# A planner that knows when VectorE and GpSimd block each other, and that plans TensorE's attention products later

## The chip, the core and the metric

The kernel runs on one core of one Trainium2 chip. The metric is the device time of one execution in microseconds (us), as the median of several runs. The engines named below are TensorE (PE in the profile, with its weight loads as PEld), VectorE (DVE), ScalarE (ACT), GpSimd (POOL) and SyncE (SP), which here only issues transfers. Each engine works through its own instructions in their order; an instruction that waits for another engine holds up all that stand behind it on its own.

## The reference: what is computed

Sliding-window attention (8 batches, 8 heads, 576 positions, head dimension 64, window 64), whose output goes as 4608 tokens of 512 features through a feed-forward layer with a rational activation. All is float32.

```python
scores = np.where((rel >= 0) & (rel < 64), scale * q @ k.T, -1e9)
attn = softmax(scores)                     # exp(scores - max) / (sum + 1e-9)
x = (attn @ v), heads side by side         # 4608 x 512
h = x @ w_in                               # 4608 x 2048
P = a[0] + a[1] * h + a[2] * h2 + a[3] * h3
Q = 1.0 + abs(b[0]) * abs(h) + abs(b[1]) * h2
out = (P / (Q + 1e-6)) @ w_out             # 4608 x 512
```

## The kernel before

**Tiles.** The tokens are cut into 12 chunks of 384. Of each chunk, attention makes x in four *units* (`plan_unit`), one per pair of heads. The feed-forward layer then goes over the chunk in 16 *steps* (`plan_gate`, `plan_out`), one per 128 of the 2048 inner features: 192 steps in all. Chunks 0 to 2 take their first eight steps first and the other eight afterwards, since the weights are still arriving and being decoded; their partial outputs are spilled and merged. From chunk 3 on a chunk takes its 16 steps in one go.

**Three products for one.** TensorE multiplies a number as the sum of a high and a low part. So x is kept as xh and xl, the gate as gh and gl, the weights as wi_h, wi_l, wo_h, wo_l, and each product is made of three matmuls. The weights come as 64-bit numbers and are decoded (`plan_decode`) by two ScalarE operations, one of GpSimd (L237) and three of VectorE (L241, L246, L257) for each of 32 tiles.

**A unit** goes: scores on TensorE into the PSUM tile ps_s (L335); masked to SBUF by VectorE (sm, L341; in chunks 1 and 2 the mask is added by TensorE instead, L327); maxima (nmx, VectorE, L352); six exponentials with sums (ScalarE, L364); inverse sums (rs, VectorE, L368 and L369); normalisation of sm (GpSimd, L373); six transposes on TensorE, again into ps_s (L378); their copy pT to SBUF (ScalarE, L382); 24 small products with V into ps_x (TensorE, L388); xh (ScalarE, L393) and xl (VectorE, L397).

**A step** goes: twelve h products into the PSUM tile h, of which there are two buffers (TensorE, L437); ah = |h|, a first num and a first u (ScalarE, L443, L446, L449); num times h twice (VectorE, L452, L455: the last reader of h); u times ah (GpSimd, L459); logarithm and exponential of u, which make 1/Q in ah (ScalarE, L462, L465); gh, a product u, the remainder num, and gl = num times ah (VectorE, L469, L473, L477, L482); then nine o products, three for each of three token tiles, of gl and gh with the output weights, into PSUM tiles that hold the sum over the chunk's 16 steps (TensorE, L520). The buffers for gh and gl number three, for ah, u and num two.

**What sets the order.** No loop does: each operation is registered in a `Plan` with its engine, a planned duration, a rank, what it comes after and which buffers it takes. `Plan.order` then plays the program through with these durations. Again and again it looks at every engine for the operations whose buffers and inputs are there, takes those that could start within 0.02 us of the earliest, among these the lowest rank, and of all engines the one that starts first. Operations are issued in the order of their planned starts. The plan decides only the order: on the chip each instruction waits on semaphores for what it needs. So a planned duration that is wrong makes an order that fits the chip less well, and never a wrong result.

**What the plan knows of VectorE and GpSimd.** Some VectorE operations (three of the decode, gh, the product u, the remainder num) are marked `shares`. Where GpSimd is busy when such an operation is to start, half of the overlap is added to its duration. gl (L482) and all others are planned at their bare duration.

Of the kernel before, what the change touches and what calls it, by code (L numbers as in the profile page):

```python
# [27 lines left out]
class Slot:  # L28


    def __init__(self, pool):
        self.pool, self.uses = pool, []


class Op:
    def __init__(self, engine, cost, rank, emit, after, uses, shares):
        self.engine, self.cost, self.rank, self.emit, self.after, self.shares = engine, cost, rank, emit, after, shares
        self.start = self.end = None
        self.takes = [s for s in uses if not s.uses]
        for s in uses:  # L40
            s.uses.append(self)


class Plan:
# [9 lines left out]
    def add(self, engine, cost, rank, emit, after=(), uses=(), shares=False):  # L54
        op = Op(engine, cost, rank, emit, [o for o in after if o is not None], list(uses), shares)
        self.ops.append(op)
        return op

    def order(self):
# [8 lines left out]
        held = {}  # L68
# [5 lines left out]
        while len(done) < len(self.ops):  # L74
            best = None
            for e in ENGINES:
                able = []
                for op in ready[e]:
                    if any(not slots[s.pool] for s in op.takes):
                        continue  # L80
                    t = max([free[e], op.ready] + [min(slots[s.pool]) for s in op.takes])
                    able.append((t, op))
                if not able:
                    continue
                t0 = min(t for t, _ in able)
                t, op = min(((t, op) for t, op in able if t <= t0 + 0.02), key=lambda x: (x[1].rank, x[0]))
                if best is None or t < best[0]:
                    best = t, op
            t, op = best
# [4 lines left out]
            if op.shares and free["POOL"] > t:  # L94
                cost += 0.5 * min(cost, free["POOL"] - t)
            op.start, op.end = t, t + cost
            if op.engine == "SP":
                self.bus = max(t, getattr(self, "bus", 0.0)) + op.cost
                op.end = self.bus + 2.0
                free["SP"] = t + 0.06  # L100
            else:
                free[op.engine] = op.end - self.TAIL[op.engine]
# [20 lines left out]
def swa_rational_ffn(ctx: ExitStack, tc: tile.TileContext, qT, kT, v, w_in, w_out, a, b, out):  # L123
# [79 lines left out]
    HA = 8  # L203
    NU = HP
# [15 lines left out]
    def plan_decode(src, hi, lo, rank):  # L220
# [41 lines left out]
        o = plan.add("POOL", 1.75, rank, sign, [o], [st])  # L262
        o = plan.add("DVE", 0.685, rank, put_sign, [o], [st, sc], True)
        o = plan.add("DVE", 0.685, rank, put_low, [o], [st, sc], True)
        o = plan.add("ACT", 0.635, rank, high, [o], [sc])
        return plan.add("DVE", 0.685, rank, rest, [o], [sc], True)
# [14 lines left out]
    def plan_unit(c, hp, rank):  # L281
# [118 lines left out]
        def link(kind, op):  # L400
            chain[kind] = op
            return op
# [11 lines left out]
        o = plan.add("POOL", 1.58, r(6), normalise, [o], [ssm])  # L414
        o = link("transposes", plan.add("PE", 0.82, r(7), transposes, [o, chain.get("transposes")], [ssm, spt]))
        o = plan.add("ACT", 0.8, r(8), copy_pT, [o], [spt, spT])
        o = plan.add("PE", 1.1, r(9), values, [o, lv, chain.get("values")], [svt, spT, spx])
# [9 lines left out]
    def plan_gate(s):  # L427
# [63 lines left out]
        u_1 = plan.add("POOL", 1.035, r(5), u1, [u_0], [st])  # L491
        o = plan.add("ACT", 0.527, r(6), logarithm, [u_1], [st])
        o = plan.add("ACT", 0.527, r(7), inverse, [o], [st])
        g = plan.add("DVE", 0.615, r(8), g_high, [o, n2], [st, sg], True)
        o = plan.add("DVE", 0.56, r(9), product, [g], [st, sg], True)
        o = plan.add("DVE", 0.615, r(10), remainder, [o], [st], True)
        gate_done[s] = plan.add("DVE", 0.555, r(11), g_low, [o], [st, sg])
# [6 lines left out]
    def plan_out(s):  # L504
# [38 lines left out]
        for t in range(NTS):  # L543
            o = plan.add("PE", 0.855, s + LAG + 0.5 + 0.01 * t, lambda t=t: products(t),
                         [gate_done[s], tile_out[i], f2.get((s - 1, t)), f2.get((s, t - 1))], [sg, so[t]])
# [84 lines left out]
```

## Time and profile before

| | |
|---|---|
| median of 3 runs | 1034.44 us (1034.14 to 1034.7) |
| the profiled execution | 1032.78 us, of which the span from first to last instruction is 1030.8 us |
| mean granted TensorE clock | 0.982 |
| busy, share of the span | TensorE 93%, weight loads 80%, VectorE 87%, ScalarE 70%, GpSimd 36% |
| gl on VectorE (L482), 192 times | mean 930 ns |
| num times h on VectorE (L452), same size, 192 times | mean 546 ns |
| normalisation on GpSimd (L373), 48 times | mean 1630 ns |
| u on GpSimd (L459), 192 times | mean 1221 ns |

The profile is that of one execution. A row of a group names the line, the engine, the operation, the tile written and the tiles read, the number of instructions, their busy time, the mean of one, and the time for which the engine stood idle just before them with what ended the wait. Matmuls overlap each other, so the starts of successive matmuls tell more than the length of one. The lines of the changed kernel are eight higher than those before from the middle of the file on: L382 before is L390 after.

### The profile page before, as it was taken

What the parts mean: (1) busy time and instruction counts of PE and PEld (TensorE: products, weight loads), DVE (VectorE), ACT (ScalarE), POOL (GpSimd) and SP (SyncE); (2) the same over time, 40 slices, a digit from 0 to 9 for tenths busy, and PEclk for the clock granted to TensorE, in tenths of its full rate; (3) what the DMA queues carried; (4) which work ended last, traced back from release to release, by engine and by line L of the source; (5) the groups of instructions that cost most, each with busy time, mean ns of one, the idle gap of its engine ahead of it and who ended that gap; (6) DMA issues with size and microseconds to landing.
All of it is one profiled execution on the core that took longest, in us unless ns stands there. A gap on an engine that the chain in (4) does not pass through costs nothing.

```text
span 1030.8 us, 18377 instructions
## 1 busy us (share of the span) xinstructions
PE 961.4 (93%) x6640; PEld 829.2 (80%) x6640; DVE 899.2 (87%) x1538; ACT 724.8 (70%) x1735; POOL 371.1 (36%) x287
## 2 busy tenths in 40 slices
PE   4687999989999999999999999999999999999998
PEld 3566788868888888888888788888888888888997
DVE  5699999999998888888888888888888888888896
ACT  4685887767786677667767766766767776767665
POOL 4445544453233333233333333333333333332221
PEclk9598999989999999999999999999999999999999
DMA  5635424221232102111111111111211111200000
GB/s 188 188 121 150 158 80 128 62 62 45 75 122 73 47 33 69 42 44 59 44 34 43 61 46 50 62 37 37 76 30 43 63 45 33 79 16 1 32 1 31
DMA packets 39545, 67.24 MB, mean 65 GB/s; under 512 B 4640, under 2 KB 25120, under 8 KB 39456
## 3 DMA queue, kind: packets, MB, share of 16 engines
q1 hardware_dynamic: 39456, 66.08, 20.1%
q8 instruction: 52, 0.85, 0.3%
q14 instruction: 37, 0.30, 0.1%
HBM read 55.05 MB, written 11.01 MB: 64 GB/s over the span
## 4 chain that ended last, share of the span: by engine, by line
DVE 33%; PE 13%; ACT 13%; POOL 11%; issue 7%; DVEq 0%; POOLq 0%; ACTq 0%
POOL u L459 8%; PE h L437 6%; DVE gh L469 6%; PE o L520 6%; DVE u L473 6%; DVE num L477 4%; DVE gl L482 4%; DVE num L455 3%; POOL sm L373 3%; DVE sm L341 3%; ACT ah L465 3%; ACT ah L443 3%; DVE nmx L352 3%; ACT pT L382 2%; ACT ah L462 2%
## 5 line engine op out<-in xcount | busy, mean ns | idle before, releaser
L459 POOL TENSOR_TENSOR u<-u,ah 128x384 f32<-128x384 f32 x192 | 234.5, 1221 | 433.2 <-ACT u L449 388.4
L437 PE MATMUL h<-xl,wi_h 128*128 128x384 f32 x768 | 262.0, 341 | 5.1 <-ACT wi_h L254 2.9
L437 PE MATMUL h<-xh,wi_l 128*128 128x384 f32 x768 | 260.0, 339 | 1.2 <-DVE wi_l L257 1.2
L437 PE MATMUL h<-xh,wi_h 128*128 128x384 f32 x768 | 259.6, 338 | 0.0
L462 ACT ACTIVATE ah<-u 128x384 f32<-128x384 f32 x192 | 101.0, 526 | 216.1 <-POOL u L459 215.9
L520 PE MATMUL o<-wo_h,gl 128*128 128x512 f32 x576 | 238.9, 415 | 6.9 <-ACT wo_h L254 4.9
L520 PE MATMUL o<-wo_l,gh 128*128 128x512 f32 x576 | 228.2, 396 | 4.5 <-DVE wo_l L257 4.4
L520 PE MATMUL o<-wo_h,gh 128*128 128x512 f32 x576 | 228.3, 396 | 0.0
L469 DVE SCALAR_TENSOR_TENSOR gh<-num,a_sb,ah 128x384 fp32r<-128x384 f32 x192 | 123.2, 642 | 78.3 <-ACT ah L465 70.0
L482 DVE TENSOR_TENSOR gl<-num,ah 128x384 fp32r<-128x384 f32 x192 | 178.5, 930 | 2.2
L437 PEld LDWEIGHTS h<-xl,wi_h 128*128 128x128 f32 x768 | 145.7, 190 | 18.1 <-DVE num L455 5.2
L437 PEld LDWEIGHTS h<-xh,wi_h 128*128 128x128 f32 x768 | 145.7, 190 | 7.1
L373 POOL TENSOR_TENSOR sm<-sm,rs 128x768 f32<-128x768 f32 x48 | 78.3, 1630 | 194.0 <-DVE rs L369 175.3
L437 PEld LDWEIGHTS h<-xh,wi_l 128*128 128x128 f32 x768 | 145.5, 189 | 2.2 <-DVE wi_l L257 2.2
L520 PEld LDWEIGHTS o<-wo_h,gl 128*128 128x128 f32 x576 | 108.6, 189 | 34.0 <-ACT wo_h L254 5.6
L449 ACT ACTIVATE u<-ah,b_sb 128x384 f32<-128x384 f32 x192 | 135.8, 707 | 0.0
L477 DVE SCALAR_TENSOR_TENSOR num<-num,a_sb,u 128x384 f32<-128x384 f32 x192 | 130.0, 677 | 2.0
L446 ACT ACTIVATE num<-h,a_sb 128x384 f32<-128x384 f32 x192 | 128.1, 667 | 0.0
L520 PEld LDWEIGHTS o<-wo_h,gh 128*128 128x128 f32 x576 | 109.0, 189 | 23.8
L520 PEld LDWEIGHTS o<-wo_l,gh 128*128 128x128 f32 x576 | 109.2, 190 | 21.6 <-DVE wo_l L257 6.4
L473 DVE SCALAR_TENSOR_TENSOR u<-u,gh 128x384 f32<-128x384 f32 x192 | 108.8, 567 | 13.1
L455 DVE SCALAR_TENSOR_TENSOR num<-num,a_sb,h 128x384 f32<-128x384 f32 x192 | 116.6, 607 | 2.4
(50 smaller groups left out, 1117.0 us busy)
## 6 DMA issues: line engine op xcount, KB each, us to landing
out<-ob SPq DMA_DIRECT2D x36, 256.0 KB, 2.0
w_st<-w_in SPq DMA_DIRECT2D x16, 512.0 KB, 3.8
w_st<-w_out SPq DMA_DIRECT2D x16, 512.0 KB, 3.8
q<-qT SPq DMA_DIRECT2D x32, 192.0 KB, 2.4
vt<-v SPq DMA_DIRECT2D x16, 384.0 KB, 3.4
vt<-v SPq DMA_DIRECT2D x16, 320.0 KB, 2.9
kt<-kT SPq DMA_DIRECT2D x16, 224.0 KB, 2.6
kt<-kT SPq DMA_DIRECT2D x16, 192.0 KB, 2.5
```

Of the source, the lines that this page charges most:

```text
L373: nc.gpsimd.tensor_tensor(out=sm, in0=sm, in1=u["rs"].unsqueeze(2).broadcast_to([P, NR, P]), op=ALU.mult)
L437: nc.tensor.matmul(h, w[:, cc, i * P:(i + 1) * P], x[c, cc], start=n == 0, stop=n == 3 * NCC - 1)
L446: nc.scalar.activation(d["num"], d["h"], AF.Identity, scale=a_sb[:, 3:4], bias=a_sb[:, 2:3])
L449: nc.scalar.activation(d["u"], d["ah"], AF.Identity, scale=b_sb[:, 1:2], bias=b_sb[:, 0:1])
L455: nc.vector.scalar_tensor_tensor(out=d["num"], in0=d["num"], scalar=a_sb[:, 1:2], in1=d["h"], op0=ALU.add, op1=ALU.mult)
L459: nc.gpsimd.tensor_tensor(out=d["u"], in0=d["u"], in1=d["ah"], op=ALU.mult)
L462: nc.scalar.activation(d["ah"], d["u"], AF.Ln, bias=QADD)
L469: nc.vector.scalar_tensor_tensor(out=d["gh"], in0=d["num"], scalar=a_sb[:, 0:1], in1=d["ah"], op0=ALU.add, op1=ALU.mult)
L473: nc.vector.scalar_tensor_tensor(out=d["u"], in0=d["u"], scalar=QADD, in1=d["gh"].bitcast(F32), op0=ALU.add, op1=ALU.mult)
L477: nc.vector.scalar_tensor_tensor(out=d["num"], in0=d["num"], scalar=a_sb[:, 0:1], in1=d["u"], op0=ALU.add, op1=ALU.subtract)
L482: nc.vector.tensor_tensor(out=d["gl"], in0=d["num"], in1=d["ah"], op=ALU.mult)
L520: nc.tensor.matmul(acc[t], g[:, ts], w[:, i, :], start=first and n == 0, stop=last and n == 2)
```

## The change

It touches the planner alone; the operations, their number and their sizes are the same.

- `shares` gives way to `port`. GpSimd's operations have a class: 0 for the one of the decode (one tensor in), 1 for the two with two tensors in (normalisation, u). The plan keeps apart until when GpSimd is busy with either class.
- VectorE's operations that had `shares` have a pair of factors instead: so much of the overlap with class 0 and with class 1 is added to their duration.
- gl has `"wait"`: while an operation of class 1 is planned on GpSimd, gl's earliest start is put 0.1 us before that one's end. Another VectorE operation that could start sooner goes ahead of it.
- The planned duration of the normalisation is 1.63 instead of 1.58 us, that of u on GpSimd 1.15 instead of 1.035 us.
- `late`: the transposes and the products with V are planned at the earliest 0.3 us after their inputs in chunks 0 to 2, and 1.5 us from chunk 3 on; the o products half as much.

```diff
-            if op.shares and free["POOL"] > t:
-                cost += 0.5 * min(cost, free["POOL"] - t)
+            if isinstance(op.port, tuple):
+                cost += sum(k * max(0.0, min(cost, b - t)) for k, b in zip(op.port, busy))
             op.start, op.end = t, t + cost
+            if op.engine == "POOL":
+                busy[op.port] = op.end
...
-                    t = max([free[e], op.ready] + [min(slots[s.pool]) for s in op.takes])
+                    t = max([free[e], op.ready + op.late] + [min(slots[s.pool]) for s in op.takes])
+                    if op.port == "wait" and busy[1] > t:
+                        t = busy[1] - 0.1
...
+    SLACK = 0.3, 1.5
...
-        o = plan.add("POOL", 1.75, rank, sign, [o], [st])
-        o = plan.add("DVE", 0.685, rank, put_sign, [o], [st, sc], True)
-        o = plan.add("DVE", 0.685, rank, put_low, [o], [st, sc], True)
+        o = plan.add("POOL", 1.75, rank, sign, [o], [st], 0)
+        o = plan.add("DVE", 0.685, rank, put_sign, [o], [st, sc], (0.55, 0.5))
+        o = plan.add("DVE", 0.685, rank, put_low, [o], [st, sc], (0.55, 0.5))
...
-        o = plan.add("POOL", 1.58, r(6), normalise, [o], [ssm])
-        o = link("transposes", plan.add("PE", 0.82, r(7), transposes, [o, chain.get("transposes")], [ssm, spt]))
+        o = plan.add("POOL", 1.63, r(6), normalise, [o], [ssm], 1)
+        o = link("transposes", plan.add("PE", 0.82, r(7), transposes, [o, chain.get("transposes")], [ssm, spt], late=SLACK[c >= C0]))
         o = plan.add("ACT", 0.8, r(8), copy_pT, [o], [spt, spT])
-        o = plan.add("PE", 1.1, r(9), values, [o, lv, chain.get("values")], [svt, spT, spx])
+        o = plan.add("PE", 1.1, r(9), values, [o, lv, chain.get("values")], [svt, spT, spx], late=SLACK[c >= C0])
...
-        u_1 = plan.add("POOL", 1.035, r(5), u1, [u_0], [st])
+        u_1 = plan.add("POOL", 1.15, r(5), u1, [u_0], [st], 1)
...
-        g = plan.add("DVE", 0.615, r(8), g_high, [o, n2], [st, sg], True)
-        o = plan.add("DVE", 0.56, r(9), product, [g], [st, sg], True)
-        o = plan.add("DVE", 0.615, r(10), remainder, [o], [st], True)
-        gate_done[s] = plan.add("DVE", 0.555, r(11), g_low, [o], [st, sg])
+        g = plan.add("DVE", 0.615, r(8), g_high, [o, n2], [st, sg], (0.6, 0.42))
+        o = plan.add("DVE", 0.56, r(9), product, [g], [st, sg], (0.35, 0.16))
+        o = plan.add("DVE", 0.615, r(10), remainder, [o], [st], (0.6, 0.18))
+        gate_done[s] = plan.add("DVE", 0.555, r(11), g_low, [o], [st, sg], "wait")
...
-                         [gate_done[s], tile_out[i], f2.get((s - 1, t)), f2.get((s, t - 1))], [sg, so[t]])
+                         [gate_done[s], tile_out[i], f2.get((s - 1, t)), f2.get((s, t - 1))], [sg, so[t]], late=SLACK[c >= C0] / 2)
```

More of the change, by code (lines that the diff above doesn't have):

```diff
@@ L35, with __init__ @@
 class Op:
-    def __init__(self, engine, cost, rank, emit, after, uses, shares):
-        self.engine, self.cost, self.rank, self.emit, self.after, self.shares = engine, cost, rank, emit, after, shares
+    def __init__(self, engine, cost, rank, emit, after, uses, port, late):
+        self.engine, self.cost, self.rank, self.emit, self.after = engine, cost, rank, emit, after
+        self.port, self.late = port, late
         self.start = self.end = None
@@ L52, in __init__, with add @@
         self.sizes, self.ops = sizes, []
-    def add(self, engine, cost, rank, emit, after=(), uses=(), shares=False):
-        op = Op(engine, cost, rank, emit, [o for o in after if o is not None], list(uses), shares)
+    def add(self, engine, cost, rank, emit, after=(), uses=(), port=None, late=0.0):
+        op = Op(engine, cost, rank, emit, [o for o in after if o is not None], list(uses), port, late)
         self.ops.append(op)
@@ L67, in order @@
         slots = {p: [0.0] * n for p, n in self.sizes.items()}
-        held = {}
+        held, busy = {}, [0.0, 0.0]
         for op in self.ops:
@@ L261, in plan_decode @@
         o = plan.add("ACT", 0.68, rank, scale, [o], [st, sc])
-        o = plan.add("POOL", 1.75, rank, sign, [o], [st])
-        o = plan.add("DVE", 0.685, rank, put_sign, [o], [st, sc], True)
-        o = plan.add("DVE", 0.685, rank, put_low, [o], [st, sc], True)
+        o = plan.add("POOL", 1.75, rank, sign, [o], [st], 0)
+        o = plan.add("DVE", 0.685, rank, put_sign, [o], [st, sc], (0.55, 0.5))
+        o = plan.add("DVE", 0.685, rank, put_low, [o], [st, sc], (0.55, 0.5))
         o = plan.add("ACT", 0.635, rank, high, [o], [sc])
-        return plan.add("DVE", 0.685, rank, rest, [o], [sc], True)
+        return plan.add("DVE", 0.685, rank, rest, [o], [sc], (0.55, 0.5))
     xh, xl = {}, {}
```

## The prediction, made before the changed kernel was run

> **What bounds the kernel now.** I read the table of stretches first, because one average over the span mixes stages with different limits. Its columns are busy time (and count) of PE, PEld, DVE, ACT and POOL, then the granted clock, DMA share and GB/s.
>
> ```profile
> 0.00:60.00 60.00, 35.18 (x370) 29.28 (x374) 38.48 (x68) 36.90 (x114) 28.72 (x32) 0.80 0.55 176
> 60.00:120.00 60.00, 48.80 (x418) 39.37 (x408) 57.72 (x95) 44.50 (x123) 31.99 (x21) 0.94 0.45 139
> 120.00:180.00 60.00, 59.13 (x376) 51.28 (x375) 59.79 (x105) 47.96 (x103) 30.08 (x21) 1.00 0.38 120
> 180.00:240.00 60.00, 53.56 (x241) 44.14 (x240) 58.14 (x99) 41.27 (x76) 29.97 (x20) 0.94 0.18 53
> 240.00:1031.00 791.00, 764.74 (x5252) 665.11 (x5251) 685.11 (x1175) 554.14 (x1324) 250.31 (x194) 1.00 0.15 48
> ```
>
> There are two regimes. From 60 to 240 us VectorE is busy 57.72 + 59.79 + 58.14 = 175.65 of 180 us: it sets the pace while weights are decoded. From 240 us on TensorE is busy 764.74 of 791 us at full clock and VectorE only 685.11. So the second regime is TensorE's, and what it loses there is what it waits for. The waits of TensorE and of its weight loads from 240 us on, as total, times and longest:
>
> ```profile
> PE ps_x L388 <- ACT pT L382: 20.9, 32, 1.1
> PE ps_s L378 <- POOL sm L373: 0.8, 2, 0.4
> ...
> PEld ps_x L388 <- ACT pT L382: 34.8, 32, 1.6
> PEld ps_s L378 <- POOL sm L373: 8.3, 32, 0.7
> PEld h L437 <- DVE num L455: 0.3, 1, 0.3
> ```
>
> TensorE is idle 791 - 764.74 = 26.3 us there, and 20.9 of it is one wait: 32 times, once per attention unit, the products with V (L388) stand for the copy of the transposed probabilities (pT, L382). The chain of waits shows one such round:
>
> ```profile
> 505.83 0.99 POOL sm L373
> 506.83 0.62 issue
> 507.45 1.33 POOL u L459
> 508.78 0.02 issue
> 508.81 0.02 ACT ah L462
> 508.83 0.41 issue
> 509.24 0.47 ACT ah L443
> 509.71 0.70 ACT pT L382
> 510.40 0.04 issue
> 510.45 0.92 PE ps_x L388 x24
> ```
>
> pT does not wait for its own input there. It stands in ScalarE's queue behind a gate step's logarithm (L462), which waits for GpSimd's u (L459), which stands behind GpSimd's normalisation (sm, L373). The rows of TensorE in that round, and of an earlier unit (254 us) in which nothing was waited for:
>
> ```profile
> 507.12 0.34 PE L437 MATMUL h<-xh,wi_h 128*128 128x384 f32 x1
> 507.29 0.34 PE L437 MATMUL h<-xh,wi_l 128*128 128x384 f32 x1
> 507.54 0.87 PE L378 MATMUL ps_s<-ident,sm 128*128 128x128 f32 x6
> 508.17 0.48 PE L520 MATMUL o<-wo_h,gl 128*128 128x512 f32 x1
> ...
> 509.41 0.40 PE L520 MATMUL o<-wo_h,gh 128*128 128x512 f32 x1
> 510.45 0.92 PE L388 MATMUL ps_x<-pT,vt 128*64 128x64 f32 x24 [0.64 <-ACT pT L382]
> ...
> 254.09 0.40 PE L520 MATMUL o<-wo_h,gh 128*128 128x512 f32 x1
> 254.41 0.39 PE L388 MATMUL ps_x<-pT,vt 128*64 128x64 f32 x6
> ```
>
> From the start of the last o product to the start of the products with V it is 510.45 - 509.41 = 1.04 us with the wait and 254.41 - 254.09 = 0.32 us without: 0.72 us lost per unit. The transposes start 0.25 us behind the last h product (507.54 - 507.29), where the next product follows after 0.17 (507.29 - 507.12): 0.08 us lost.
>
> **The change, part one: products later.** Transposes and products with V are planned at the earliest 1.5 us after their inputs from chunk 3 on (0.3 before), o products half of that. No instruction is added; the order moves. On TensorE around the 30th unit, before (ps_s<-ident,sm are the transposes, ps_x the products with V):
>
> ```order
> L378 MATMUL ps_s<-ident,sm 128x128 x6
> L520 MATMUL o_6240<-wo_h,gl 128x512
> L520 MATMUL o_6240<-wo_l,gh 128x512
> L520 MATMUL o_6240<-wo_h,gh 128x512
> L520 MATMUL o_6246<-wo_h,gl 128x512
> L520 MATMUL o_6246<-wo_l,gh 128x512
> L520 MATMUL o_6246<-wo_h,gh 128x512
> L388 MATMUL ps_x<-pT,vt 64x64 x12
> ```
>
> and now, around the 31st unit (the h rows go on to twelve):
>
> ```order
> L528 MATMUL o_6214<-wo_h,gl 128x512
> L528 MATMUL o_6214<-wo_l,gh 128x512
> L528 MATMUL o_6214<-wo_h,gh 128x512
> L445 MATMUL h<-xl_2_5213,wi_h 128x384
> L445 MATMUL h<-xh_2_5203,wi_h 128x384
> ...
> L445 MATMUL h<-xh_2_5848,wi_l 128x384
> L396 MATMUL ps_x<-pT,vt 64x64 x12
> ```
>
> What moved: before, two groups of o products lie between the transposes and the products with V. Now one whole group of twelve h products lies there as well. What such groups last stands in the chain:
>
> ```profile
> 512.27 2.08 PE h L437 x12
> 514.35 2.06 PE o L520 x9
> ```
>
> Nine o products take 2.06, so a group of three takes 0.69 us; the cover was 2 x 0.69 = 1.38 us and becomes 1.38 + 2.08 = 3.46 us. In the order of the change it is 3.46 us for 26 of the 35 units from the 14th on, and 2.77 us (one o group and the h group) for four. Against the 0.72 us that were missing, 1.4 to 2.1 us are added, and the transposes themselves come later by the same slack: from a unit's scores to its products with V the orders put 9.65 us of h and o groups before and 11.7 to 19.3 now, so everything on the way, from the masked scores to pT, has more time. On ScalarE the copy has moved too. Before, around pT:
>
> ```order
> L364 ACTIVATE sm,sums<-sm,nmx 128x128 x6
> L443 ACTIVATE ah<-h 128x384
> L446 ACTIVATE num<-h,a_sb 128x384
> L449 ACTIVATE u<-ah,b_sb 128x384
> L462 ACTIVATE ah<-u 128x384
> L443 ACTIVATE ah<-h 128x384
> L382 COPY pT<-ps_s 128x768
> ```
>
> and now, with one more gate step between the exponentials (L372) and pT:
>
> ```order
> L372 ACTIVATE sm,sums<-sm,nmx 128x128 x6
> L470 ACTIVATE ah<-u 128x384
> L451 ACTIVATE ah<-h 128x384
> L473 ACTIVATE ah<-ah 128x384
> L454 ACTIVATE num<-h,a_sb 128x384
> L457 ACTIVATE u<-ah,b_sb 128x384
> L470 ACTIVATE ah<-u 128x384
> L473 ACTIVATE ah<-ah 128x384
> L390 COPY pT<-ps_s 128x768
> ```
>
> So pT still stands behind a logarithm and one more short ScalarE step (L473 where L443 was). If it is late, that is not cured on ScalarE but covered on TensorE.
>
> The gain: 32 x 0.72 = 23.0 us for the products with V, 32 x 0.08 = 2.6 for the transposes, together 25.6. Bounds: the idle time alone gives 20.9 + 0.8 = 21.7, the idle time of the weight loads 34.8 + 8.3 = 43.1, which loads ahead would partly have hidden. I take 25.6, which rests on starts of matmuls.
>
> **Part one costs.** The units are no longer evenly spaced, so h groups come at less even distances. The h of a step needs the PSUM buffer of the step two before, whose last reader is num (L455). I counted the h and o groups that the orders put between the end of an h and the start of the one after the next, at the durations above and without the attention products, which add cover. Before it is 6.2 us at all 142 steps from the 48th on; in the change it is 4.8 us at 13 of them, 5.5 at 41, 6.2 at 35 and more at the rest. How late num is, from the rows of VectorE:
>
> ```profile
> 506.19 1.71 DVE L482 TENSOR_TENSOR gl<-num,ah 128x384 fp32r<-128x384 f32 x1
> 507.82 0.54 DVE L452 TENSOR_TENSOR num<-num,h 128x384 f32<-128x384 f32 x1
> 508.40 0.61 DVE L455 SCALAR_TENSOR_TENSOR num<-num,a_sb,h 128x384 f32<-128x384 f32 x1
> ...
> 512.35 0.61 DVE L455 SCALAR_TENSOR_TENSOR num<-num,a_sb,h 128x384 f32<-128x384 f32 x1
> ```
>
> The h group that ended at 507.29 + 0.34 = 507.63 had its num at 512.96, 5.33 us later. So the 13 steps could wait 0.5 us each and the others not: between 0 (attention products lie between, or num comes sooner) and 6.5 us. I take 3, the middle. Late products cost nothing else: the o products stand further behind their h than before, 13.1 to 16.6 us of such work where it was 12.4, so gl, which every o group needs, has more time.
>
> **Part two: steering around GpSimd.** The gl row at 506.19 shows what is meant: gl takes 1.71 us because it started in GpSimd's normalisation (row below, to 507.48) and ended at 507.90. The planner now does not start gl (L482) while a GpSimd operation with two tensors runs, unless nothing else is ready; gh, u and num of the remainder are only given another price.
>
> ```profile
> 505.83 1.65 POOL L373 TENSOR_TENSOR sm<-sm,rs 128x768 f32<-128x768 f32 x1 [4.33 <-DVE rs L369]
> ```
>
> Where that could pay, by means per operation, 60 to 240 us ahead and 300 to 900 us behind:
>
> ```profile
> L477 DVE SCALAR_TENSOR_TENSOR num<-num,a_sb,u 128x384 f32<-128x384 f32 x32 | 29.1, 911 | 0.0
> L469 DVE SCALAR_TENSOR_TENSOR gh<-num,a_sb,ah 128x384 fp32r<-128x384 f32 x31 | 22.0, 710 | 0.2 <-ACT ah L465 0.2
> L482 DVE TENSOR_TENSOR gl<-num,ah 128x384 fp32r<-128x384 f32 x32 | 18.2, 569 | 0.0
> ...
> L482 DVE TENSOR_TENSOR gl<-num,ah 128x384 fp32r<-128x384 f32 x119 | 122.8, 1032 | 2.0
> L477 DVE SCALAR_TENSOR_TENSOR num<-num,a_sb,u 128x384 f32<-128x384 f32 x119 | 73.3, 616 | 1.0
> ```
>
> gl loses 119 x (1.032 - 0.569) = 55 us, but in the regime in which VectorE is busy 685 of 791 us and TensorE sets the end: worth 0 by itself, hidden under TensorE's products (if TensorE stood still, up to those 55). Where VectorE does set the pace, gl loses almost nothing (569 ns) and num loses 32 x (0.911 - 0.616) = 9.4 us; num is not kept away. I take 0 for that stretch. Bounds: all of num's 9.4 us and as much again on gh and the decode gone, -19; the same again added by a poorer order there, +19.
>
> The Trainium skill ("SBUF — State Buffer", section "Who interferes with whom") speaks against the prices: an operation with two SBUF inputs and a GpSimd operation that reads SBUF lock each other out, and the later one blocks until the first has finished. The trace agrees: gl ends 0.42 us after the normalisation. The planner's prices of 0.18 and 0.16 of the overlap for num and u are too low by that rule; by it the sum would be that of case (d) below, by the rows above it is the 0.
>
> **Sum.** The profiled execution took 1032.78 us (span 1030.8 and 2.0 around it); its order gives 1032.8 - 25.6 + 3 + 0 = 1010.2. The runs' median is 1034.44, 1.7 above it: 1011.9, so 1012.
>
> **Rivals.** (a) Half of the wait stays, because pT still stands behind L470 and L473: 1012 + 13 = 1025. For it: the order of ScalarE; against it: 3.46 us of cover where 1.38 + 0.72 were needed. (b) VectorE's stretch gets shorter too, by half of the bound: 1012 - 10 = 1002. For it: 175.65 of 180 us busy; against it: the rule steers gl alone, which lost nothing there. (c) Slower: h waits for num in the second regime. If num came 6.2 us behind its h, which the old distances still cover, the new ones would be short of it by 13 x 1.4 + 41 x 0.7 = 46.9 us: 1034.4 - 25.6 + 46.9 = 1056. It decides from about 5.8 us on (13 x 1.0 + 41 x 0.3 = 25.3), where the waits eat the whole gain. For it: 5.33 is not far off. Against it: that round had gl blocked for 1.1 us just ahead of num, and attention products add cover at many of these places. (d) No gain: in VectorE's stretch, collisions pass from gl to gh, u and num, which are not kept away. If in every second one of its 32 steps one more of them is blocked as gl was (1.71 - 0.57 = 1.14 us), that adds 16 x 1.14 = 18: 1030, and 1034 with 19 such steps.
>
> **How the numbers follow.** Forecast 0.61 (1012, by itself 1005 to 1019), (a) 0.12, (b) 0.14, (c) 0.08, (d) 0.05. A difference under 0.2% (2.1 us) can't be told from none. Faster by more: 0.61 + 0.12 + 0.14 and a small part of (d), 0.87; same 0.04 from (d); slower 0.09 from (c) and the rest of (d). The range leaves out (c), (d) and the far end of (b): 998 to 1028.
>
> **What would show it.** After 240 us the wait of L396 for pT is under 5 us in all (20.9 now), TensorE is busy 99% there (764.74 of 791 us now, 97%), and gl's mean falls below 0.8 us. Wrong would be: new waits of h (L445) for num of over 10 us, waits of o products for gl or gh of over 5, or a stretch with VectorE over 95% busy that ends 10 us later than now.

## The result, and the profile after

| | median, us | ratio to before (95%) | profiled span, us |
|---|---|---|---|
| before | 1034.29 (1032.66 to 1034.7) | | 1030.8 |
| after | 1041.0 (1039.56 to 1042.17) | 1.0067 (1.005 to 1.0085) | 1040.3 |

The change makes the kernel slower by 0.7%. The forecast was 1012 us, 2.2% faster: wrong in sign, and the result lies outside its range. Yet what the change was to remove is gone. The stretches of the profile after (columns as in the prediction):

```profile
60.00:240.00 180.00, 160.25 (x1004) 133.57 (x1003) 170.23 (x287) 130.26 (x292) 91.45 (x61) 0.95 0.33 102
240.00:1040.00 800.00, 777.55 (x5277) 667.76 (x5275) 669.75 (x1189) 557.53 (x1333) 232.89 (x196) 1.00 0.15 47
```

The waits of TensorE from 240 us on:

```profile
PE h L445 <- DVE num L463: 12.2, 24, 1.6
PE o L528 <- DVE gl L490: 2.5, 3, 1.1
PE ps_s L343 <- ACT pT L390: 2.0, 2, 1.1
PE o L528 <- DVE wo_l L265: 1.8, 2, 1.2
```

and of its weight loads:

```profile
PEld h L445 <- DVE num L463: 32.9, 56, 2.0
```

The wait of the products with V for pT, 20.9 us before, no longer appears. In its place the h products wait for num, 24 times. To see where the time went I followed one instruction through both traces, the start of ah = |h| of a step on ScalarE (L443 before, L451 after), which comes 192 times. The timeline of before, steps 0, 48, 172 and 191:

```profile
48.88 0.52 ACT L443 ACTIVATE ah<-h 128x384 f32<-128x384 f32 x1
...
312.47 0.49 ACT L443 ACTIVATE ah<-h 128x384 f32<-128x384 f32 x1 [0.81 <-PE h L437]
...
939.76 0.49 ACT L443 ACTIVATE ah<-h 128x384 f32<-128x384 f32 x1 [0.20 <-DVE gl L482]
...
1018.29 0.49 ACT L443 ACTIVATE ah<-h 128x384 f32<-128x384 f32 x1 [0.29 <-PE h L437]
```

and of after:

```profile
53.17 0.49 ACT L451 ACTIVATE ah<-h 128x384 f32<-128x384 f32 x1 [0.64 <-PE h L445]
...
318.86 0.49 ACT L451 ACTIVATE ah<-h 128x384 f32<-128x384 f32 x1 [0.25 <-DVE gl L490]
...
942.74 0.49 ACT L451 ACTIVATE ah<-h 128x384 f32<-128x384 f32 x1 [0.64 <-DVE gl L490]
...
1027.82 0.49 ACT L451 ACTIVATE ah<-h 128x384 f32<-128x384 f32 x1 [0.64 <-DVE gl L490]
```

Three differences come out, and they add up to the 9.5 us by which the span grew (1040.3 - 1030.8):

- **Start:** step 48 begins 318.86 - 312.47 = 6.4 us later, and 53.17 - 48.88 = 4.3 us of that are there at step 0. Part of it is scatter between executions: the medians lie 6.7 us apart, the two profiled executions 9.5, and xh_tmp2 below, with the orders of after on every engine, has the same middle (623.9 us) and end (97.6) but begins step 48 at 315.8.
- **Middle:** steps 48 to 172 take 623.9 us where they took 627.3. The gain that was to be 22 us and more is 3.4.
- **End:** from step 172 on it takes 1040.3 - 942.74 = 97.6 us where it took 1030.8 - 939.76 = 91.0, 6.5 us more.

The brackets of the last three rows of after name the same releaser: ah waited for gl. ah, u and num have two buffers, and gl is the last reader of ah and num, so the first operation of a step waits for the last one of two steps earlier. The waits of ScalarE for this from 240 us on, before:

```profile
ACT ah L443 <- DVE gl L482: 10.8, 35, 2.4
```

and after:

```profile
ACT ah L451 <- DVE gl L490: 72.4, 87, 2.3
```

VectorE in turn now stands still for ScalarE's first num, which it did not before:

```profile
DVE num L460 <- ACT num L454: 52.1, 51, 1.5
```

What this makes of the steps is seen in the chain of waits of after, one turn around 620 us:

```profile
617.93 0.57 DVE gl L490
618.54 0.04 issue
618.59 0.49 ACT ah L451
619.08 0.57 ACT num L454
619.67 0.55 DVE num L460
620.23 0.53 DVE gh L477
620.75 0.06 DVE num L463
620.82 0.38 issue
621.20 0.85 DVE u L481
622.07 0.63 DVE num L485
622.72 0.57 DVE gl L490
623.33 0.04 issue
623.37 0.49 ACT ah L451
```

No row of TensorE is in it: from gl to ah, through num, back to gl, and again to ah. The turn takes 623.37 - 618.59 = 4.78 us, more than the 4.15 us that steps without attention products take at the end of before (table below). TensorE has no attention product in this turn, and its next h products stand still for num (L463):

```profile
621.34 0.44 PE L445 MATMUL h<-xl,wi_h 128*128 128x384 f32 x1 [0.21 <-DVE num L463]
```

In the chain, gl (617.93) frees the buffers for ah of two steps later. In VectorE's queue that later step's num (619.67) stands ahead of gh, u, num and gl of the step between, so these wait too, and their gl frees the next buffers.

Last, VectorE and GpSimd. The groups of VectorE between 300 and 900 us of which the prediction did not show the rows before:

```profile
L469 DVE SCALAR_TENSOR_TENSOR gh<-num,a_sb,ah 128x384 fp32r<-128x384 f32 x119 | 73.5, 618 | 65.3 <-ACT ah L465 58.6 <-PE h L437 2.5
...
L473 DVE SCALAR_TENSOR_TENSOR u<-u,gh 128x384 f32<-128x384 f32 x120 | 66.8, 557 | 9.9
```

and after:

```profile
L485 DVE SCALAR_TENSOR_TENSOR num<-num,a_sb,u 128x384 f32<-128x384 f32 x120 | 88.0, 734 | 2.0
...
L477 DVE SCALAR_TENSOR_TENSOR gh<-num,a_sb,ah 128x384 fp32r<-128x384 f32 x120 | 83.5, 696 | 26.0 <-ACT ah L473 11.8 <-PE o L528 5.9 <-PE ps_s L386 4.2
...
L481 DVE SCALAR_TENSOR_TENSOR u<-u,gh 128x384 f32<-128x384 f32 x120 | 81.4, 678 | 5.8
...
L490 DVE TENSOR_TENSOR gl<-num,ah 128x384 fp32r<-128x384 f32 x119 | 67.0, 563 | 1.5
```

gl fell from 1032 to 563 ns as planned. But gh rose by 78, u by 121 and num by 118 ns (734 against 616), together 317 of the 469 ns by which gl became shorter. Counted in the traces from 300 to 900 us, 87 of these four operations start inside an operation of GpSimd before, 86 of them gl; after, 106 do: 33 gh, 36 u, 34 num and 3 gl.

### The profile page after: what moved, and what is told of

It reads as the page before. It is cut to its first block, busy times and chain, and to the rows that moved or that the text cites. A ratio compares the mean times of both kernels' runs of the same rounds, so it can differ in the third digit from the quotient of the medians.

```text
span 1040.3 us, 18366 instructions
## 1 busy us (share of the span) xinstructions
PE 972.1 (93%) x6640; PEld 829.5 (80%) x6640; DVE 876.0 (84%) x1538; ACT 724.0 (70%) x1735; POOL 354.4 (34%) x287
## 4 chain that ended last, share of the span: by engine, by line
DVE 36%; PE 25%; ACT 15%; issue 7%; POOL 3%; DMA 0%; POOLq 0%; DVEq 0%; ACTq 0%
PE h L445 11%; PE o L528 10%; DVE u L481 8%; DVE num L485 7%; DVE gh L477 6%; DVE num L460 4%; DVE num L463 4%; ACT sm L372 4%; DVE gl L490 4%; ACT num L454 3%; ACT ah L451 3%; POOL u L467 2%; ACT ah L473 2%; ACT ah L470 1%; ACT u L457 1%
## 5 line engine op out<-in xcount | busy, mean ns | idle before, releaser
L467 POOL TENSOR_TENSOR u<-u,ah 128x384 f32<-128x384 f32 x192 | 218.2, 1138 | 472.9 <-ACT u L457 418.4
L445 PE MATMUL h<-xl,wi_h 128*128 128x384 f32 x768 | 267.0, 348 | 20.1 <-DVE num L463 19.6
L477 DVE SCALAR_TENSOR_TENSOR gh<-num,a_sb,ah 128x384 fp32r<-128x384 f32 x192 | 131.7, 686 | 36.7 <-ACT ah L473 19.9
L451 ACT ACTIVATE ah<-h 128x384 f32<-128x384 f32 x192 | 94.1, 490 | 90.7 <-DVE gl L490 79.2
L460 DVE TENSOR_TENSOR num<-num,h 128x384 f32<-128x384 f32 x192 | 105.3, 549 | 52.3 <-ACT num L454 52.1
L485 DVE SCALAR_TENSOR_TENSOR num<-num,a_sb,u 128x384 f32<-128x384 f32 x192 | 146.1, 761 | 2.6
L481 DVE SCALAR_TENSOR_TENSOR u<-u,gh 128x384 f32<-128x384 f32 x192 | 127.7, 666 | 7.8
L381 POOL TENSOR_TENSOR sm<-sm,rs 128x768 f32<-128x768 f32 x48 | 74.7, 1557 | 162.4 <-DVE rs L377 84.6
```

What stands on the lines that cost most here:

```text
L381: nc.gpsimd.tensor_tensor(out=sm, in0=sm, in1=u["rs"].unsqueeze(2).broadcast_to([P, NR, P]), op=ALU.mult)
L445: nc.tensor.matmul(h, w[:, cc, i * P:(i + 1) * P], x[c, cc], start=n == 0, stop=n == 3 * NCC - 1)
L451: nc.scalar.activation(d["ah"], d["h"], AF.Abs)
L460: nc.vector.tensor_tensor(out=d["num"], in0=d["num"], in1=d["h"], op=ALU.mult)
L467: nc.gpsimd.tensor_tensor(out=d["u"], in0=d["u"], in1=d["ah"], op=ALU.mult)
L477: nc.vector.scalar_tensor_tensor(out=d["gh"], in0=d["num"], scalar=a_sb[:, 0:1], in1=d["ah"], op0=ALU.add, op1=ALU.mult)
```

## What the experiments were to tell apart

The first theory was that the wait for buffers took the place of the wait for pT, because the steered gl holds them longer: with two buffers of ah, u and num the steps can go only as fast as the loop in the chain above. Rivals were that the late products alone do the harm, by uneven distances of the h groups; that the late o products are what does it; that the part on VectorE and GpSimd does it; and that the order of num and gh in VectorE's queue does it. The table has all kernels; the sections behind it say what each is. "Start" is when ah of step 0 begins, "48" when that of step 48 does; "per step" is the mean distance over steps 50 to 172, "at the end" over steps 174 to 190. "Behind gl" counts, out of 122 steps in the middle, how often ah starts within 0.12 us of the end of gl two steps back. All are worked out from the starts of ah (and ends of gl) in each trace.

| kernel | median, us | ratio (95%) | start | 48 | per step | at the end | behind gl |
|---|---|---|---|---|---|---|---|
| before | 1034.29 | | 48.9 | 312.5 | 5.05 | 4.15 | 30 |
| after | 1041.0 | 1.0067 (1.005 to 1.0085) | 53.2 | 318.9 | 5.03 | 4.50 | 95 |
| late_only | 1051.28 | 1.0174 (1.0159 to 1.0189) | 54.1 | 320.1 | 5.11 | 4.54 | 100 |
| port_only | 1017.15 | 0.9843 (0.9828 to 0.9858) | 49.1 | 316.1 | 4.89 | 4.15 | 47 |
| xh_tmp2 | 1040.28 | 1.0064 (1.0049 to 1.0079) | 54.2 | 315.8 | 5.03 | 4.50 | 95 |
| xh_tmp3 | 1025.83 | 0.9928 (0.9911 to 0.9945) | 54.1 | 313.4 | 4.96 | 4.25 | |
| no_o_late | 1030.64 | 0.997 (0.9957 to 0.9982) | 53.8 | 320.0 | 5.01 | 4.07 | 52 |
| o_late_only | 1032.84 | 0.9996 (0.9986 to 1.0006) | 48.8 | 316.3 | 4.97 | 4.47 | 92 |
| port_nowait | 1025.99 | 0.9929 (0.9914 to 0.9944) | 49.8 | 318.1 | 4.96 | 4.14 | 53 |
| tv_late_old | 1046.66 | 1.0132 (1.0116 to 1.0147) | 54.1 | 323.1 | 5.09 | 4.11 | 46 |
| tv_steady | 1028.07 | 0.9952 (0.9937 to 0.9966) | 48.5 | 316.2 | 5.00 | 4.07 | 54 |
| tv_small | 1040.29 | 1.0072 (1.0057 to 1.0087) | 49.1 | 313.7 | 5.11 | 4.14 | 32 |
| port_xh_tmp3 | 1005.37 | 0.9735 (0.9719 to 0.9751) | 49.4 | 309.6 | 4.84 | 4.15 | |
| dur_only | 1026.0 | 0.9932 (0.9917 to 0.9946) | 49.7 | 317.0 | 4.95 | 4.15 | 53 |
| after_gfirst | 1051.14 | 1.0174 (1.0159 to 1.0189) | 54.2 | 318.2 | 5.13 | 4.35 | 83 |
| port_gfirst | 1045.63 | 1.0127 (1.011 to 1.0143) | 49.9 | 319.2 | 5.10 | 4.09 | 82 |
| no_o_tmp3 | 1019.38 | 0.9868 (0.9853 to 0.9883) | 52.7 | 315.8 | 4.91 | 4.15 | |

With three buffers a step takes its buffers from three steps back, so the last column has no entry there. Nine of the fifteen times behind before and after lie outside every range that was expected for them: late_only, port_only, no_o_late, o_late_only, port_nowait, tv_late_old, tv_small and both gfirst kernels.

## Each part alone: late products, and the rules for VectorE and GpSimd

late_only keeps the late products and takes the planner's rules and durations of before:

```diff
-                    if op.port == "wait" and busy[1] > t:
-                        t = busy[1] - 0.1
...
-            if isinstance(op.port, tuple):
-                cost += sum(k * max(0.0, min(cost, b - t)) for k, b in zip(op.port, busy))
+            if isinstance(op.port, tuple) and free["POOL"] > t:
+                cost += 0.5 * min(cost, free["POOL"] - t)
...
-        o = plan.add("POOL", 1.63, r(6), normalise, [o], [ssm], 1)
+        o = plan.add("POOL", 1.58, r(6), normalise, [o], [ssm], 1)
...
-        u_1 = plan.add("POOL", 1.15, r(5), u1, [u_0], [st], 1)
+        u_1 = plan.add("POOL", 1.035, r(5), u1, [u_0], [st], 1)
```

> Of the change only the later planning of TensorE's products (0.3 and 1.5 us, o products half); durations and the half-overlap rule for GpSimd are those of before. Theory P (steering gl holds the two buffers of ah, u and num longer, and the next step's ah waits for gl): with the steering gone the gain of some 22 us after 240 us shows, 1012 to 1022 us. Theory L (lateness lets h products run ahead of the gates into their two PSUM buffers): as slow as the change, 1036 to 1045 us, with over 8 us of h products waiting for num after 240 us.

port_only keeps the rules and plans no product late:

```diff
-    SLACK = 0.3, 1.5
+    SLACK = 0.0, 0.0
```

> Of the change only the new rules and prices for VectorE and GpSimd; no product is planned late. Theory P: the waits for pT come back and the buffer waits stay, 1036 to 1055 us, ah waits for gl over 50 us in all. Theory L: 1025 to 1036 us, h waits for num under 5 us after 240 us.

Measured: late_only 1051.28 us, slower by 1.7%; port_only 1017.15 us, faster by 1.6%, and the fastest of the kernels that compute everything. So the part that I forecast to bring the gain loses 17 us on the old rules and 1041.0 - 1017.15 = 23.9 on the new ones, and the part that I priced at nothing wins 17 us. gl is steered in port_only too, so steering is not what makes the buffers too few. The waits of TensorE from 240 us on, port_only:

```profile
PE ps_s L386 <- POOL sm L381: 4.3, 6, 1.6
PE ps_x L396 <- ACT pT L390: 1.2, 2, 0.6
...
PE h L445 <- DVE num L463: 0.8, 2, 0.4
```

The wait for pT goes from 20.9 to 1.2 us here without any late product, and h does not take its place. In late_only it does:

```profile
PE h L443 <- DVE num L461: 23.9, 33, 1.3
```

## The buffers of ah, u and num

A third buffer takes 4.5 KB of SBUF per partition (three tiles of 384 float32). Two kernels make room for it by leaving out the low part of x: their h products use xh in its place, in as many matmuls of the same size. One of them keeps two buffers, to show what that alone does, the other has three. The plan counts two in both, so the order of the instructions is the same on every engine:

```diff
-            xl[c, hp] = xp.tile([P, CH], F32R, name=f"xl{hp}_{slot_of[c]}", bufs=1)
+            xl[c, hp] = xp.tile([P, CH], F32R, name="xl")
...
-                for w, x in ((wi_h, xl), (wi_h, xh), (wi_l, xh)):
+                for w, x in ((wi_h, xh), (wi_h, xh), (wi_l, xh)):
...
-    tmp = ctx.enter_context(tc.tile_pool(name="tmp", bufs=2))
+    tmp = ctx.enter_context(tc.tile_pool(name="tmp", bufs=3))
```

(the last two lines in xh_tmp3 alone)

> The changed kernel in the same order, with xh read in place of xl in the h products and xl written to a scratch tile, which frees memory; the low part of x is so left out of the h products. Control for the next one. Both theories: 1038 to 1043 us, as the change, since TensorE reads a tile of the same size.

> As the control, with three buffers of ah, u and num in place of two; the order of the instructions is the same on every engine. The low part of x is left out as there. If the two-step loop ah -> ... -> gl -> ah of the step after the next sets the pace after 320 us (its 9.7 + 0.3 us are two steps of 4.98 us), the h waits for num fall from 12 to under 4 us there and the time to 1015 to 1030 us. If the h products are simply too early for num, whatever ah waits for, the time stays within 4 us of the control.

Measured: 1040.28 us with two buffers, as after, and 1025.83 with three: 14.5 us less. The wait of h for num, two buffers:

```profile
PE h L445 <- DVE num L463: 12.2, 24, 1.5
```

three buffers:

```profile
PE h L445 <- DVE num L463: 6.0, 11, 1.5
```

So waiting for the buffers costs 14 us of the time of after, 10 of them between steps 48 and 172 (623.9 against 613.8 us), and half of the wait of h. Since the order is the same, this is the price of the waits and not of another order. It is not the whole: with three buffers the kernel is still 8.7 us slower than port_only with two.

The same on port_only (port_xh_tmp3, three buffers and xh for xl):

> No lateness at all, new rules for VectorE and GpSimd, xh in place of xl in the h products (so the low part of x is left out of them) and three buffers of ah, u and num. Without lateness TensorE waits only 9 us in all after 240 us, so if the two-buffer loop limits only the late kernels, the third buffer gives under 4 us: 1012 to 1018 us. If it limits every order, as much as in the late one (14 us): 1000 to 1006 us.

Measured: 1005.37 us, 11.8 less than port_only, 4.84 us per step. Its stretch from 240 us on:

```profile
240.00:1003.00 763.00, 758.43 (x5246) 664.73 (x5245) 664.14 (x1172) 546.77 (x1322) 225.48 (x194) 1.00 0.16 50
```

TensorE is busy 758.43 of 763 us, 99.4%. This is the state that the prediction expected of the change: TensorE with nothing to wait for. Steps 48 to 172 take 601.8 us, 25.5 less than before (627.3). So 4.84 us per step is about what TensorE itself needs, and all orders with two buffers stay above it, port_only by 0.05 us, before by 0.21.

This pair also corrects the first theory. The third buffer helps the order without lateness almost as much (11.8 us) as that of after (14.5). With three buffers late products still cost 1025.83 - 1005.37 = 20.5 us, where they cost 23.9 with two; between steps 48 and 172 they cost 613.8 - 601.8 = 12.0 us, where it is 623.9 - 607.6 = 16.2 with two. So the two buffers bind in after, but most of what lateness costs stays without them. Of the 12.0 us, 5.1 are h standing for num.

## Which late products

In no_o_late the transposes and the products with V stay late, the o products do not; in o_late_only it is the other way round; tv_late_old is late_only without late o products:

```diff
-                         [gate_done[s], tile_out[i], f2.get((s - 1, t)), f2.get((s, t - 1))], [sg, so[t]], late=SLACK[c >= C0] / 2)
+                         [gate_done[s], tile_out[i], f2.get((s - 1, t)), f2.get((s, t - 1))], [sg, so[t]], late=0.0)
```

(no_o_late and, on late_only, tv_late_old)

```diff
-        o = link("transposes", plan.add("PE", 0.82, r(7), transposes, [o, chain.get("transposes")], [ssm, spt], late=SLACK[c >= C0]))
+        o = link("transposes", plan.add("PE", 0.82, r(7), transposes, [o, chain.get("transposes")], [ssm, spt], late=0.0))
...
-        o = plan.add("PE", 1.1, r(9), values, [o, lv, chain.get("values")], [svt, spT, spx], late=SLACK[c >= C0])
+        o = plan.add("PE", 1.1, r(9), values, [o, lv, chain.get("values")], [svt, spT, spx], late=0.0)
```

(o_late_only)

> The change without the lateness of the o products; transposes and products with V stay late. h groups are again 6.2 us of h and o work apart at 140 of 142 steps. Theory O (the lateness of the o products makes the distances of the h products uneven, so that they meet the two-buffer loops of h and of ah, u, num): 1005 to 1018 us, h waits for num under 3 us after 240 us, the last 16 steps back at 4.15 us each. Theory TV (late transposes and products with V do it): 1034 to 1042 us.

> The change with the lateness of the o products alone; transposes and products with V as early as before. Theory O: 1034 to 1048 us, the last 16 steps at 4.4 to 4.6 us, h waits for num over 8 us after 240 us. Theory TV: 1012 to 1022 us, as without any lateness (1017).

> Durations and overlap rule of before, transposes and products with V late (0.3 and 1.5 us), o products not. h groups are 6.2 us apart at 140 of 142 steps, and 3.5 us of work lie between transposes and products with V. If the pT wait was worth what the prediction priced it at: 1009 to 1016 us, pT waits under 3 us. If another limit stands right behind it (the loop over two buffers of ah, u, num: 8.8 us per two steps and more): 1020 to 1034 us.

Measured: 1030.64, 1032.84 and 1046.66 us. Against port_only, late transposes and products with V cost 13.5 us, late o products 15.7, both together 23.9. So neither alone is guilty, and the theory that the o products are the whole cause fell. What the o products cost is the more uniform: with them the last steps take 4.47 to 4.54 us, without them 4.07 to 4.15, in three pairs (o_late_only against port_only, after against no_o_late, late_only against tv_late_old). Over 19 steps that is 6 to 8 us. There no attention is left that could fill the gap, which would explain it but was not tried. In after, TensorE stands from step 172 on for gl (2.5 us) and for num (2.4), in port_only for gl alone (0.3): 4.6 of the 6.3 us by which the end is longer (97.6 against 91.3). With three buffers it is still 96.3 us against 91.3. The late o products also put ah behind gl in 92 to 100 of 122 steps, where it is 46 to 52 without. The waits of ScalarE from 240 us on, o_late_only:

```profile
ACT ah L451 <- DVE gl L490: 76.8, 94, 2.7
```

In tv_late_old the products with V do not wait for pT either, but the transposes wait for the normalisation, 16.1 us in 29 times. The last of the group, no_o_tmp3, is no_o_late with three buffers and xh for xl:

> Transposes and products with V late, o products not, with xh in place of xl in the h products (the low part of x is left out of them) and three buffers of ah, u and num. If the 13 us that late transposes and products with V cost between steps 48 and 172 come through the two-buffer loop: 4.85 to 4.90 us per step there in place of 5.01, 1008 to 1016 us in all. If they come through the attention chain (o products wait for the copy of a finished sum, which stands behind the exponentials): 4.95 us or more, 1018 to 1028 us.

Measured: 1019.38 us, 11.3 less than with two; 4.91 us per step where port_xh_tmp3 has 4.84. So of the 0.116 us per step that late transposes and products with V cost with two buffers (5.008 against 4.892), about half is left with three (4.907 against 4.844, 0.063). More than half of this rest is a wait of TensorE that port_xh_tmp3 does not have:

```profile
PE o L528 <- ACT ob L542: 4.7, 7, 0.7
```

The o products stand for ScalarE's copy of a finished sum, which frees their PSUM tile, as the second expectation had it: 4.7 of 609.9 - 601.8 = 8.1 us between steps 48 and 172. In no_o_late with two buffers it is 7.6 us in 14 times, of 620.7 - 607.6 = 13.1. For what remains beyond these waits the runs show no cause.

## How much lateness, and where

tv_steady and tv_small are no_o_late with other numbers; in both nothing is late in chunks 0 to 2:

```diff
-    SLACK = 0.3, 1.5
+    SLACK = 0.0, 1.5
```

(tv_steady; 0.0, 0.4 in tv_small)

> The new rules for VectorE and GpSimd, o products not late, transposes and products with V late by 1.5 us from chunk 3 on and by nothing before. If the 0.3 us in the first chunks cost the 4 to 5 us that the first step starts later (ah of step 0 at 53 to 54 us in every kernel that has them, 49 in those without): ah of step 0 at 49 us and ah of step 48 some 4 us earlier than without this edit (320.0), 1025 to 1028 us. If they did not: 1029 to 1032 us.

> As the last one with 0.4 us in place of 1.5. If any lateness of transposes and products with V costs (they come later than their inputs and the one-buffer tiles ps_s, pT and ps_x are free later): 1018 to 1028 us, between none (1017) and 1.5 us. If 0.4 us only takes the waits of transposes for GpSimd (4.3 us after 240 us) and of pT (1.2 us): 1011 to 1016 us.

tv_steady: 1028.07 us, 2.6 less than no_o_late. Step 0 begins at 48.5 instead of 53.8 us and step 48 at 316.2 instead of 320.0. In the table, all eight kernels whose transposes and products with V are late by 0.3 us in chunks 0 to 2 start at 52.7 to 54.2 us, the nine others at 48.5 to 49.9: lateness of 0.3 us moves the first step by 4 to 5 us. The path is TensorE's queue. In tv_steady the h products of step 0 stand ahead of the next unit's transposes and start right behind the products with V:

```profile
43.68 1.23 PE L396 MATMUL ps_x<-pT,vt 128*64 128x64 f32 x24
44.84 0.44 PE L445 MATMUL h<-xl,wi_h 128*128 128x384 f32 x1
```

In no_o_late they stand behind those transposes, for which TensorE first stands still:

```profile
49.21 1.51 PE L386 MATMUL ps_s<-ident,sm 128*128 128x128 f32 x6 [2.17 <-issue]
50.37 0.67 PE L445 MATMUL h<-xl,wi_h 128*128 128x384 f32 x1
```

So they start 50.37 - 44.84 = 5.5 us later, about what step 0 loses (53.8 against 48.5). What these transposes waited for the profile does not name.

tv_small: 1040.29 us. Less lateness, and 12 us slower. The waits of TensorE from 240 us on:

```profile
PE ps_s L386 <- POOL sm L381: 21.9, 29, 1.4
```

and of ScalarE:

```profile
ACT sm L372 <- DVE nmx L360: 48.4, 33, 1.6
```

The products with V do not wait, but one place earlier the transposes wait for the normalisation as long and as often as the products with V waited for pT before (20.9 us, 32 times). The cover between transposes and products with V was there: 3.5 us in 31 units. So the time does not follow the lateness, nor that cover; each number makes another order, and each order has its own slowest place.

## The rules for VectorE and GpSimd taken apart

port_nowait is port_only without the rule for gl; dur_only is the kernel before with nothing but the two durations of GpSimd:

```diff
-        gate_done[s] = plan.add("DVE", 0.555, r(11), g_low, [o], [st, sg], "wait")
+        gate_done[s] = plan.add("DVE", 0.555, r(11), g_low, [o], [st, sg])
```

(port_nowait)

```diff
-        o = plan.add("POOL", 1.58, r(6), normalise, [o], [ssm])
+        o = plan.add("POOL", 1.63, r(6), normalise, [o], [ssm])
...
-        u_1 = plan.add("POOL", 1.035, r(5), u1, [u_0], [st])
+        u_1 = plan.add("POOL", 1.15, r(5), u1, [u_0], [st])
```

(dur_only)

> The new prices and GpSimd durations without lateness and without the rule that keeps gl out of GpSimd's operations. If the rule for gl made the 16 us of the port part (gl at 0.58 us instead of 1.04, so pT and ah come sooner): 1028 to 1036 us with gl back at 0.9 to 1.1 us and pT waits of 15 us or more. If the prices and durations made it: 1014 to 1022 us.

> The kernel before with GpSimd's planned durations of the change (1.63 and 1.15 us in place of 1.58 and 1.035) and nothing else: no new prices, no rule for gl, no lateness. If these durations made the 7 us that the prices and durations gave together: 1024 to 1029 us, pT waits of 7 to 11 us after 240 us. If the prices made it: 1031 to 1036 us, pT waits of 15 to 21.

Measured: 1025.99 and 1026.0 us. So the durations alone win 8 us, the new prices of gh, u and num nothing on top, and the rule for gl another 9. In dur_only the wait for pT is shorter each time, not rarer (8.7 us in 31 times; 20.9 in 32 before):

```profile
PE ps_x L388 <- ACT pT L382: 8.7, 31, 0.7
```

That fits what was wrong in the plan: u on GpSimd takes 1.22 us and was planned at 1.035, and its logarithm stands ahead of pT in ScalarE's queue.

## The order in VectorE's queue

In the loop of the chain, num of a later step stands ahead of gh of the step before. Both kernels forbid that: num of a step is planned behind gh of the step before.

```diff
-        n1 = plan.add("DVE", 0.553, r(4), num1, [n0], [sh, st])
+        n1 = plan.add("DVE", 0.553, r(4), num1, [n0, gh_done.get(s - 1)], [sh, st])
...
+        gh_done[s] = g
```

(gh_done starts as an empty dictionary; after_gfirst is this on after, port_gfirst on port_only)

> The change, with one more dependency in the planner alone: the first num times h of a step is planned after gh of the step before, so that it never stands ahead of it in VectorE's queue (it did at 52 of 143 steps from the 48th on; before at none). If that queue order closes the slow loop (ah of a step waits for gl two steps back, num for ah, gh stands behind num, gl behind gh): 1020 to 1032 us, the last 16 steps at 4.15 to 4.3 us in place of 4.50. If the uneven distances of the h products do it by themselves: 1036 to 1043 us, the last 16 steps at 4.4 to 4.55.

> The same dependency in the kernel without lateness, where it changes 15 steps between the 48th and the 172nd. If the queue order costs there too: 1008 to 1015 us. If TensorE's work is what is left: 1015 to 1019 us.

Measured: 1051.14 and 1045.63 us, slower by 10 and 28 us than without. The theory that this inversion is the fault found no support. It is gone from VectorE's queue (no step between the 48th and the 172nd has it; in after 46 have, in port_only 15), but in after_gfirst h now waits longer for num. The waits of TensorE, after_gfirst:

```profile
PE h L446 <- DVE num L464: 19.9, 42, 1.5
```

In port_gfirst most of the new waits are others: the transposes stand 14.2 us for the normalisation and the products with V 8.4 for pT, where it was 4.3 and 1.2 in port_only; h stands 4.8 us for num, where it was 0.8. ah starts right behind gl in 83 and 82 of 122 steps, where it was 95 and 47. The rule makes another order as a whole, so these runs show that it does not help, and not what the inversion alone costs.

## Why the prediction was wrong, point by point

- **What bounds the kernel** was read rightly as to the wait: 20.9 us for pT, gone after. What the prediction did not see is how near the next limit lay. In before, ah already stood behind gl in 30 of 122 steps, and I had listed waits of TensorE alone.
- **The gain of 25.6 us** did not come: the wait vanished, and yet steps 48 to 172 gained 3.4 us. The size was right as what TensorE loses: port_xh_tmp3, in which it waits for next to nothing, takes 25.5 us less there. The products with V were covered, as worked out. The steps that failed are the two costs that follow, what it takes to plan the products late. Signs named: the wait for pT below 5 us came true (none is listed), gl's mean below 0.8 us too (0.563 between 300 and 900 us), TensorE busy 99% did not (777.55 of 800, 97%).
- **The cost of h waiting for num** was put at 3 us, between 0 and 6.5. It is 12.2 us, 24 times, and the sign named for wrong, over 10 us, came. By starts of matmuls, as the gain was counted, it is more, about 18 us between steps 48 and 172: from an o product to an h product behind it 339 ns on average (122 times) where it was 231, within h groups 177.5 ns (1375 times) where it was 173.5. The count of h and o groups gave the distances, but num's lateness came from one round and was held fixed, while the same change makes num later: its ah waits for gl. Rival (c) had the mechanism, at 46.9 us four times too large as a wait, and missed that it is half a matter of the buffers (6.0 us with three).
- **"Late products cost nothing else"** is the sentence that the runs contradict most directly. Late products cost 17 us on the old rules and 24 on the new ones; 4 us lie ahead of step 0, 6 to 8 in the last 19 steps (4.50 against 4.07 us in after and no_o_late), neither of which I looked at, and 16 between steps 48 and 172 (after against port_only). There 12 remain with three buffers, so the loop of the chain is the smaller part of this cost. The waits of o products for gl stayed under the 5 us named (2.5), and all three of them lie behind step 172: most of the cost shows at other products than the late o products.
- **Part two at 0** was wrong by 17 us. The argument was that VectorE's losses lie hidden under TensorE. They do as sums; but planned durations of operations off the critical path decide which order the plan makes, and the two corrected ones alone took 12 us off the wait for pT (20.9 to 8.7), the rule for gl most of the rest. That a late gl delays num behind it, ScalarE behind that, and so pT, is my reading of it. Another path is open: with gl steered, GpSimd's own u takes 1071 ns on average between 300 and 900 us in port_only, 1248 in port_nowait, and its logarithm stands ahead of pT. The runs do not part the two. The bounds of -19 to +19 held the -17, but for the wrong stretch: step 48 comes no earlier in port_only (316.1 against 312.5), while the steps behind take 4.89 us instead of 5.05.
- **Rival (d)**, collisions passing from gl to gh, u and num, was forecast for the stretch up to 240 us. There it did not come: gh and num, at 710 and 911 ns before, took less, u about the same (597 and 607 ns), and VectorE was busy 170.23 of 180 us where it was 175.65. The rows of after, 60 to 240 us:

```profile
L485 DVE SCALAR_TENSOR_TENSOR num<-num,a_sb,u 128x384 f32<-128x384 f32 x31 | 27.1, 873 | 0.0
...
L477 DVE SCALAR_TENSOR_TENSOR gh<-num,a_sb,ah 128x384 fp32r<-128x384 f32 x31 | 20.1, 653 | 0.9 <-PE ps_x L396 0.8
```

  It came behind that stretch, with two thirds of the time (317 of 469 ns), and the operations that were hit stand in the loop: gh, u and num in the chain above. One instance in the timeline of after, first VectorE:

```profile
615.64 0.94 DVE L477 SCALAR_TENSOR_TENSOR gh<-num,a_sb,ah 128x384 fp32r<-128x384 f32 x1
```

and GpSimd:

```profile
615.14 1.02 POOL L467 TENSOR_TENSOR u<-u,ah 128x384 f32<-128x384 f32 x1 [2.83 <-ACT u L457]
```

gh ends at 616.58, 0.42 us after GpSimd's u (616.16), as gl did behind the normalisation before. The Trainium skill ("SBUF — State Buffer", section "Who interferes with whom") says that two such operations lock each other out and the later one waits for the earlier to finish; the trace agrees: gh, 618 ns on average before, took 0.94 us. By that rule the prediction priced its case (d), in the stretch where it did not come. The gh, u and num that start inside an operation of GpSimd in after end 0.41 us behind it in the median.

What stays open: what the transposes ahead of step 0 wait for, by which path the rule for gl shortens the wait for pT, and the part of the cost of late products that is neither a wait for buffers nor one of those listed.

## What to carry to other kernels

Where a plan fixes the order of several engines' queues, a wait on the busiest engine is one of several loops of nearly the same length; before pricing its removal, list the waits of the other engines on the same tiles and ask how many buffers back each one reaches, since the next loop may lie within a per cent (5.052 us per step before, 5.025 after, with quite different waits). Mend the plan's durations from the profile before adding slack: two corrected numbers won 8 us, and slack of the same kind lost 24. A constant that is added for the middle of a program is to be priced at its start and end as well, where there is less other work to cover it.

## What was not expected of the hardware

Moving gl out of GpSimd's way passed two thirds of the time on to its neighbours in the queue, in more collisions than before (106 against 87), and by the same rule each: the operation that comes later ends about 0.41 us after GpSimd's. That steering nevertheless won 9 us in port_only, where VectorE's lost time was not on the path that sets the end, was not expected; the profile shows that TensorE's wait for pT went with it, from 8.9 us in port_nowait to 1.2:

```profile
PE ps_x L396 <- ACT pT L390: 8.9, 33, 0.3
```
